# A seven-product matmul scheme with running PSUM sums, and seven quarter products for one of its products

## Chip, cores and metric

The kernel runs on one core of a Trainium2 chip. The metric is device time in microseconds, from the first to the last instruction with what lies around it; smaller is better. All matmuls are fp32.

## The reference

Threshold attention over 8 batches x 8 heads of 576 tokens (head size 64), then a routed two-layer network over 4608 tokens: 512 to 1024 to 512 features, 8 experts, each token with one expert.

```python
scores = scale * np.matmul(q, k.transpose(0, 1, 3, 2))
thresh = np.max(scores, axis=-1, keepdims=True) - tau
scores = np.where(scores >= thresh, scores, -1000000000.0)
attn = softmax(scores)                      # exp and division by the sum + 1e-9
x = (attn @ v) as (4608, 512)
expert_idx = token_ids * 2654435761 % 8
out[mask_e] = np.maximum(x[mask_e] @ w1[e], 0.0) @ w2[e]
```

The lines on softmax and on x are shortened here. The change touches the last line alone.

## The kernel before

**Stages.** The first half is attention, with the first layer of expert 0 done in its gaps. The expert stage follows: layer 2 of expert 0, then layers 1 and 2 of experts 1 to 7. Experts are taken in order of their number of tokens; each has a fixed number of places, 544 for expert 0, 576 for experts 1 to 4, 600 for 5 to 7 (caps). Activations are kept with features on partitions and tokens along the free side, so a weight block is the stationary operand of a matmul and half of the tokens (272, 288 or 300 columns; 240 in layer 2 of expert 7, whose other 120 tokens are done by last_tile) the moving one.

**Seven products.** Each layer is cut in 2 x 2 blocks (rows of w, columns of w, halves of the tokens), and seven (line 926) makes it of seven block products in place of eight. Four sums of weight blocks (left: s1 to s4) and four of activation blocks (right: t1 to t4) are made first by VectorE; s1 overwrites a21, t1 overwrites b12. The products are a11 b11, a12 b21, s2 t2, s3 t3, a22 t4, s1 t1, s4 b22. Each goes to a fresh pair of PSUM banks (bank2, line 851, which alternates between two pools of two pairs each), and VectorE adds it to what was added before: ScalarE copies p1 to SBUF, VectorE makes c11, u2, u3, c21, u4, c22 and c12, seven adds, and ScalarE applies the ReLU in layer 1. Layer 1 runs seven for two groups of 256 output features (14 products of 4 fp32 matmuls); layer 2 runs it once (7 products of 8). Every fp32 matmul is a pair of instructions in the trace, so a product shows as x8 or x16. In the profile L941 is the matmul of seven, L951 the copy of p1, L948 the ReLU, L861 the helper add (the seven adds, and s1), L858 the helper sub (the other sums of blocks).

**Operands.** In layer 1 the 128 columns of a weight block lie side by side (w1_blocks). In layer 2, except for expert 7, the features are dealt (dealt, line 877): output feature m of block i comes from every fourth column of w_sb, so a stationary operand reads fp32 values 16 bytes apart, and from w_s, the sums, 8 bytes apart. Dealt features let VectorE transpose the result oT in 32 x 32 squares into o_q (put_squares, line 1024), from which POOL writes rows of the output by indirect DMA.

**Order around it.** The order of instructions on each engine is the written one (manual_schedule). seven calls a hook after each output or sum (after): side1 in layer 1 (line 1085), side2 in layer 2 (line 1099). The hooks deal out VectorE's other work: sums of w2 and h for the coming layer 2 (w2_work, h_work), sums of w1 and x for the next expert (x_work), the squares of the next expert's x (turn_x, line 1052: five transpositions into xq, then 16 DMAs on SP that carry xq to xT), put_squares; and POOL's gathers (fetch), SP's weight loads (load_w1, load_w2). At the end put_out and last_tile write expert 7's rows.

Of the kernel before, what the change touches and what calls it, by code (L numbers as in the profile page):

```python
# [20 lines left out]
def kernel(  # L21
# [805 lines left out]
    with tc.tile_pool(name="m_x", bufs=1) as m_x, \  # L827
         tc.tile_pool(name="m_o", bufs=3) as m_o, \
# [9 lines left out]
        o_end = m_x.tile([P, DIN], FP32, name="o_end")  # L838
# [6 lines left out]
        halves = [m_s.tile([P, 2, CH], FP32, name=n) for n in ("p1", "u2", "u3", "u4")]  # L845
# [3 lines left out]
        turn = [0]  # L849

        def bank2():
            turn[0] ^= 1
            if turn[0]:
                return ps_sc.tile([P, 2, 512], FP32, name="sc")
            return ps_m.tile([P, 2, 512], FP32, name="bank2")
# [53 lines left out]
        def sums_w2(e):  # L909
            s1 = None  # L910
            if e == E - 1:
                spare = w_pool.tile([P, CO, F], FP32, name="w1_sb")
                s1 = w_tiles["s1"] = spare[:, :, 0:D2]
            return left(*w2_blocks(e, w_tiles[e, 2]), w2_sums(e), s1)
# [11 lines left out]
        def seven(a, a_s, b, b_s, m0, outs, relu, after):  # L926

            (a11, a12, s1, a22), (s2, s3, s4) = a, a_s
            (b11, t1, b21, b22), (t2, t3, t4) = b, b_s
            c11, c12, c21, c22 = outs  # L930
            n_k, width, dealt_out = a11.shape[1], b11.shape[2], len(a11.shape) == 4
            p1, u2, u3, u4 = (t[:, :, 0:width] for t in halves)

            def product(x, y):
                ps = bank2()
                for i in range(2):
                    c0 = m0 + P * i
                    for c in range(n_k):
                        lhsT = (x[:, c, :, i] if dealt_out else
                                x[:, c, c0:c0 + P])  # L940
                        nc.tensor.matmul(ps[:, i, 0:width], lhsT=lhsT, rhs=y[:, c],  # L941
                                         start=c == 0, stop=c == n_k - 1)
                return ps[:, :, 0:width]

            def out(c, ps, u, step):
                add(c, ps, u)()
                if relu:
                    nc.scalar.activation(c, c, AF.Relu)  # L948
                after(step)

            nc.scalar.copy(p1, product(a11, b11))  # L951
            out(c11, product(a12, b21), p1, 0)
# [244 lines left out]
```

## Time and profile before

| | us |
|---|---|
| median of 3 runs | 931.19 (930.16 to 933.33) |
| profiled execution | 931.3 |
| its span | 929.7 |
| expert stage in it: first product of layer 2 of expert 0 to last_tile | 501.02 to 914.19 |
| one layer of experts 1 to 4 without waits (14 x 1.94 or 7 x 3.88) | 27.16 |
| one layer of experts 5 to 7 without waits (layer 2 of expert 7 is shorter) | 28.28 |

The page gives the busy time of each engine and, in 40 slices of 23 us, its share in tenths; a group line gives line of the code, engine, operation, operands, shapes and count, then total, mean ns and idle time before it; a timeline line gives start, length, engine, line, operands and count, and in brackets how long the engine stood before it and for whom. PEld is the weight load, which runs ahead beside PE. Lengths of matmuls are longer than their pitch, as they overlap: times per product are taken from start to start.

### The profile page before, as it was taken

Reading aid. Unit: us, or ns where it says so; the run is one execution under the profiler, and the core shown is the slowest. Engines: PE = TensorE matmul, PEld = TensorE weight load, DVE = VectorE, ACT = ScalarE, POOL = GpSimd, SP = SyncE. Lnnn points to the kernel's source line nnn. Section 1 sums busy time; section 2 is a strip of 40 time slices with the busy share of each in tenths; the row PEclk is TensorE's granted clock in tenths of the full one; section 3 lists DMA queues with packets and bytes.
Section 4 is the critical chain, followed back from the end, with each engine's and each line's share of the span. In section 5 each row is a group of like instructions: output and inputs, shape, how many; then the busy total and the mean of one; then the engine's idle time right before and its main releaser. Section 6 shows DMA issues by size and latency. Waiting matters only on the chain.

```text
span 929.7 us, 20725 instructions
## 1 busy us (share of the span) xinstructions
PE 909.8 (98%) x7495; PEld 662.0 (71%) x7495; DVE 757.5 (81%) x1654; ACT 457.3 (49%) x741; POOL 403.7 (43%) x528
## 2 busy tenths in 40 slices
PE   7999999999999999999999999999999999999996
PEld 4666666656666566665678888788887978878785
DVE  7999999999999999999955776767668676777551
ACT  6888888888888898888812010110201021020110
POOL 4232432456666623455423370724527073440702
PEclk9999999999999999999999999999999999999999
DMA  7354463554545668743101745364372536412101
GB/s 175 92 148 118 109 152 93 136 131 103 123 105 153 159 165 214 216 107 88 30 25 51 237 131 158 133 173 141 95 223 75 164 133 165 157 34 50 48 3 55
DMA packets 114775, 113.11 MB, mean 122 GB/s; under 512 B 32475, under 2 KB 89315, under 8 KB 114672
## 3 DMA queue, kind: packets, MB, share of 16 engines
q1 hardware_dynamic: 105168, 92.64, 37.0%
q0 software_dynamic: 9072, 18.91, 7.0%
q8 instruction: 61, 1.00, 0.4%
q14 instruction: 42, 0.34, 0.1%
q10 hardware_dynamic: 432, 0.21, 0.1%
HBM read 81.99 MB, written 21.44 MB: 111 GB/s over the span
## 4 chain that ended last, share of the span: by engine, by line
PE 65%; issue 21%; POOL 7%; DVE 3%; ACT 2%; DMA 1%; another core or an unknown queue 1%; POOLq 0%; SPq 0%; DVEq 0%; ACTq 0%
PE av L313 18%; PE sc L235 15%; PE tr L282 11%; PE sc L941 9%; PE bank L941 8%; POOL out_dram L1036 6%; PE sc L640 2%; PE av L282 1%; POOL xg L119 1%; ACT w L260 1%; DVE ns L246 1%; DVE w L271 1%; ACT wT_b L303 1%; ACT wT_a L303 0%
## 5 line engine op out<-in xcount | busy, mean ns | idle before, releaser
L260 ACT ACTIVATE w<-ns,nmx 128x576 f32<-128x576 f32 x288 | 220.5, 777 | 28.8 <-DVE ns L246 27.8
L271 DVE SCALAR_TENSOR_TENSOR w<-ns,thr,w 128x576 f32<-128x576 f32 x288 | 225.8, 816 | 0.0
L1036 POOL DMA_INDIRECT out_dram<-o_q,qidx x127 | 138.1, 1087 | 191.7 <-DVE o_q L1028 153.1
L246 DVE TENSOR_SCALAR_CACHE_REDUCE ns<-sc 128x576 f32<-128x576 f32 x288 | 205.6, 747 | 8.1 <-PE sc L235 7.4
L253 POOL TENSOR_SCALAR thr<-nmx,drop 128x2 f32<-128x2 f32 (+1 forms) x160 | 104.4, 653 | 187.3 <-DVE ns L246 177.6
L235 PE MATMUL sc<-k_sb,q 64*128 64x288 f32 (+1 forms) x1280 | 179.2, 423 | 1.0 <-DVE drop L704 0.7
L282 PEld LDWEIGHTS tr<-ident,w 64*128 64x128 f32 x2624 | 106.0, 138 | 95.4 <-ACT wT_b L303 32.4
L282 PE MATMUL tr<-ident,w 64*128 64x64 f32 x2624 | 139.5, 231 | 6.0 <-ACT wT_b L303 2.6
L948 ACT ACTIVATE h<-h 128x576 f32<-128x576 f32 (+1 forms) x56 | 38.7, 693 | 164.8 <-DVE h L861 126.1
L235 PEld LDWEIGHTS sc<-k_sb,q 64*128 64x128 f32 (+1 forms) x1280 | 93.0, 177 | 23.2 <-DVE ns L246 9.4
L313 PE MATMUL av<-wT_a,v 128*64 128x320 f32 (+1 forms) x704 | 100.6, 418 | 0.2
L303 ACT COPY wT_a<-tr 128x512 f32<-128x512 f32 (+1 forms) x128 | 81.7, 638 | 20.7 <-PE tr L282 20.2
L303 ACT COPY wT_b<-tr 128x512 f32<-128x512 f32 (+1 forms) x128 | 81.4, 636 | 17.1 <-PE tr L282 11.2
L313 PE MATMUL av<-wT_b,v 128*64 128x256 f32 x640 | 83.2, 389 | 0.0
L313 PEld LDWEIGHTS av<-wT_a,v 128*64 128x64 f32 x704 | 43.8, 137 | 29.3 <-DVE xm L352 0.7
L951 ACT COPY p<-bank 128x576 f32<-128x576 f32 (+2 forms) x11 | 7.0, 633 | 99.5 <-PE bank L941 72.5
L313 PEld LDWEIGHTS av<-wT_b,v 128*64 128x64 f32 x640 | 40.2, 136 | 18.8 <-issue 0.7
L542 POOL DMA_INDIRECT slot_scratch<-tok,slot_i x36 | 45.0, 1251 | 9.4 <-issue 7.6
L941 PE MATMUL bank<-h,w_sb 128*128 128x288 f32 (+3 forms) x192 | 48.1, 404 | 0.0
L941 PE MATMUL sc<-h,w_sb 128*128 128x288 f32 (+3 forms) x192 | 47.7, 401 | 0.0
L941 PEld LDWEIGHTS bank<-h,w_sb 128*128 128x128 f32 x192 | 46.6, 300 | 0.5
L941 PEld LDWEIGHTS sc<-h,w_sb 128*128 128x128 f32 x192 | 45.9, 289 | 0.6
(197 smaller groups left out, 1303.7 us busy)
## 6 DMA issues: line engine op xcount, KB each, us to landing
w_sb<-in_moe_w_dram SPq DMA_DIRECT2D x16, 2048.0 KB
q<-in_q_dram SPq DMA_DIRECT2D x62, 288.0 KB
v<-in_v_dram SPq DMA_DIRECT2D x32, 256.0 KB
x_scratch<-xm SPq DMA_DIRECT2D x32, 256.0 KB
xT<-xq SPq DMA_DIRECT2D x84, 80.0 KB
k_sb<-in_k_dram SPq DMA_DIRECT2D x31, 144.0 KB
k_sb<-in_k_dram SPq DMA_DIRECT2D x32, 112.0 KB
x_scratch<-xg SPq DMA_DIRECT2D x9, 256.0 KB
```

Of the source, the lines that this page charges most:

```text
L235: nc.tensor.matmul(sc[out_rows, i, 0:S2], lhsT=q_sb[rows, h, q0:q1], rhs=k_sb[rows, h], start=True, stop=True)
L246: nc.vector.tensor_scalar(out=ns[:].rearrange("p (i s) -> p i s", i=2), in0=sc[:, :, 0:S2], scalar1=-1.0, scalar2=None, op0=ALU.mult, op1= ...
L253: nc.gpsimd.tensor_scalar(out=thr[:, 0:j + 1], in0=stats[n][0][:, 0:j + 1], scalar1=drop[:], scalar2=None, op0=ALU.add)
L260: nc.scalar.activation(w, nss[n, j][:], AF.Exp, bias=stats[n][0][:, j:j + 1], scale=-1.0)
L271: nc.vector.scalar_tensor_tensor(out=w, in0=nss.pop((n, j))[:], scalar=stats[n][1][:, j:j + 1], in1=w, op0=ALU.is_le, op1=ALU.mult, accum_ ...
L282: nc.tensor.transpose(dst[:, r, 64 * c:64 * c + 64], src[rows, c0:c0 + P], ident[rows, rows])
L303: nc.scalar.copy(dst, tr[:, :, 0:64 * n_c].rearrange("p r (c q) -> p r c q", c=n_c))
L313: nc.tensor.matmul(av[64 * j:64 * j + 64, g, c0:c1], lhsT=v_sb[:, c, 64 * j:64 * j + 64], rhs=wT[g][:, i, c0:c1], start=(c == 0), stop=stop)
L542: nc.gpsimd.indirect_dma_start(out=slot_dram[c % 2][:, :], out_offset=bass.IndirectOffsetOnAxis(ap=slot_i[:, c:c + 1], axis=0), in_=tok[:, ...
L941: nc.tensor.matmul(ps[:, i, 0:width], lhsT=lhsT, rhs=y[:, c], start=c == 0, stop=c == n_k - 1)
L948: nc.scalar.activation(c, c, AF.Relu)
L1036: inst = nc.gpsimd.indirect_dma_start(out=rows[:, :], out_offset=bass.IndirectOffsetOnAxis(ap=idx, axis=0), in_=o_sb, in_offset=None, boun ...
```

## The change

Three things. First, the seven products are not each put in a fresh pair of banks: p1, u2, u3 and c21 are successive states of one pair x, onto which the products accumulate, and s1 t1 and c12 of another pair z; ScalarE copies x to SBUF after p1, u2 and u3 (u3 by halves), VectorE adds only c11, c22 and c12. The banks are four fixed pairs (banks). Second, in experts 1 to 7 the product a12 b21 is made by a class Quarters of seven products of its quarters (half the columns, half the inner rows): in layer 1 for both groups at once, in layer 2 of one output chunk each. Each of these products is 2 fp32 matmuls of half width in both layers. Their sums wi_s and bi_s are made by VectorE in the hooks, ScalarE copies their p1, s1 t1, u2 and c21 out, VectorE adds the other three results, and the whole is written into the place of c11, to which p1 is added later (join; in the second group of layer 1 first(False) adds the product from PSUM). Third, the hooks are numbered anew and deal out the work in other portions; o_sb and o_end give way to the buffers xg_bufs.

What is left out: bi_sums, inner_w, inner_b and second_blocks (views of quarters, and left and right on them), the body of the old seven, two lines on buffers of output rows and the overflow loop's output buffer.

```diff
-        o_end = m_x.tile([P, DIN], FP32, name="o_end")
...
-        halves = [m_s.tile([P, 2, CH], FP32, name=n) for n in ("p1", "u2", "u3", "u4")]
+        halves = [m_s.tile([P, 2, CH], FP32, name=n) for n in ("p1", "u2", "u3")]
+        wi_s = m_s.tile([P, 3, D2], FP32, name="wi_s")
+        bi_s = m_s.tile([P, 3, CH], FP32, name="bi_s")
+        quarters = [m_s.tile([P, CH], FP32, name=n) for n in ("q_p1", "q_u2", "q_p5")]
...
-        turn = [0]
-        def bank2():
-            turn[0] ^= 1
-            if turn[0]:
+        banks, turn = [], [0]
+        def late_tile(fo):
+            if fo in (2, 4):
                 return ps_sc.tile([P, 2, 512], FP32, name="sc")
             return ps_m.tile([P, 2, 512], FP32, name="bank2")
+        def bank2():
+            turn[0] += 1
+            return banks[(turn[0] - 1) % 4]
...
+                w_tiles["s1_q"] = spare[:, 0:2, D2:D2 + P]
...
+        def products(ps, x, y, start, mid=None):
+            for i, lhsTs in enumerate(x):
+                for c, lhsT in enumerate(lhsTs):
+                    nc.tensor.matmul(ps[:, i], lhsT=lhsT, rhs=y[:, c], start=start and c == 0,
+                                     stop=c == len(lhsTs) - 1, skip_group_check=not start)
+                if i == 0 and mid:
+                    mid()
+        def columns(x, m0=0, n=2):
+            if len(x.shape) == 4:
+                return [[x[:, c, :, i] for c in range(x.shape[1])] for i in range(n)]
+            return [[x[:, c, m0 + P * i:m0 + P * i + P] for c in range(x.shape[1])]
+                    for i in range(n)]
+        class Seven:
+            def __init__(self, a, a_s, b, b_s, m0, outs, relu, x, z):
+                self.a = [columns(t, m0) for t in (*a, *a_s)]
+                self.b, self.outs, self.relu = (*b, *b_s), outs, relu
+                width = b[0].shape[2]
+                self.x, self.z = x[:, :, 0:width], z[:, :, 0:width]
+                self.p1, self.u2, self.u3 = (t[:, :, 0:width] for t in halves)
+            def evict(self, c, src):
+                if self.relu:
+                    nc.scalar.activation(c, src, AF.Relu)
+                elif src is not c:
+                    nc.scalar.copy(c, src)
+            def out(self, c, ps, u):
+                add(c, ps, u)()
+                self.evict(c, c)
+            def first(self, keep=True):
+                products(self.x, self.a[0], self.b[0], True)
+                if keep:
+                    nc.scalar.copy(self.p1, self.x)
+                else:
+                    self.out(self.outs[0], self.x, self.outs[0])
+            def second(self, y):
+                y = y[:, :, 0:self.x.shape[2]]
+                products(y, self.a[1], self.b[2], True)
+                self.out(self.outs[0], y, self.p1)
+            def join(self):
+                self.out(self.outs[0], self.outs[0], self.p1)
+            def u2_sum(self):
+                products(self.x, self.a[4], self.b[4], False)
+                nc.scalar.copy(self.u2, self.x)
+            def s1_t1(self):
+                products(self.z, self.a[2], self.b[1], True)
+            def u3_sum(self):
+                products(self.x, self.a[5], self.b[5], False)
                 for i in range(2):
+                    nc.scalar.copy(self.u3[:, i], self.x[:, i])
+            def c22(self):
+                self.out(self.outs[3], self.z, self.u3)
+            def c21(self):
+                products(self.x, self.a[3], self.b[6], False)
+                self.evict(self.outs[2], self.x)
+            def c12(self, mid=None):
+                products(self.z, self.a[6], self.b[3], False, mid)
+                self.out(self.outs[1], self.z, self.u2)
+        class Quarters:
+            def __init__(self, a, a_s, b, b_s, outs, n, x, y, z):
+                self.a = [columns(t, 0, n) for t in (*a, *a_s)]
+                self.b, self.outs = (*b, *b_s), outs
+                width = b[0].shape[2]
+                self.x, self.y, self.z = (t[:, :, 0:width] for t in (x, y, z))
+                self.p1, self.u2, self.p5 = (
+                    t[:, 0:n * width].rearrange("p (i t) -> p i t", i=n) for t in quarters)
+            def p1_p2(self):
+                products(self.x, self.a[0], self.b[0], True)
+                nc.scalar.copy(self.p1, self.x)
+                products(self.y, self.a[1], self.b[2], True)
+                add(self.outs[0], self.y, self.p1)()
+            def s1_t1(self):
+                products(self.z, self.a[2], self.b[1], True)
+                nc.scalar.copy(self.p5, self.z)
+            def u2_sum(self):
+                products(self.x, self.a[4], self.b[4], False)
+                nc.scalar.copy(self.u2, self.x)
+            def c12(self):
+                products(self.z, self.a[6], self.b[3], False)
+                add(self.outs[1], self.z, self.u2)()
+            def c22(self):
+                products(self.x, self.a[5], self.b[5], False)
+                add(self.outs[3], self.x, self.p5)()
+            def c21(self):
+                products(self.x, self.a[3], self.b[6], False)
+                nc.scalar.copy(self.outs[2], self.x)
+        def w_quarters(a):
+            if len(a.shape) == 4:
+                return [a[:, 2 * j:2 * j + 2, :, i:i + 1] for i in range(2) for j in range(2)]
+            k, m = a.shape[1] // 2, a.shape[2] // 2
+            return [a[:, k * j:k * j + k, m * i:m * i + m] for i in range(2) for j in range(2)]
+        def wi_sums(a):
+            return [wi_s[:, i].rearrange("p (k m i) -> p k m i", k=2, i=1) if len(a.shape) == 4
+                    else wi_s[:, i].rearrange("p (k m) -> p k m", k=a.shape[1] // 2)
+                    for i in range(3)]
...
+        def quarters_of(e, layer, x, y, z):
+            a, b = second_blocks(e, layer)
+            t = b.shape[2] // 2
+            if layer == 1:
+                outs = [h_0[:, 2 * i:2 * i + 2, t * k:t * k + t] for i in range(2) for k in range(2)]
+            else:
+                outs = [oT[:, i:i + 1, t * k:t * k + t] for i in range(2) for k in range(2)]
+            a_q = w_quarters(a)
+            if (e, layer) == (E - 1, 2):
+                a_q[2] = w_tiles["s1_q"]
+            return Quarters(a_q, wi_sums(a), b_quarters(b), bi_sums(b), outs,
+                            3 - layer, x, y, z)
         def layer1(e, side):
-            w, half = w_tiles.pop((e, 1)), caps[e] // 2
-            for g in range(NG):
+            w, half = w_tiles[e, 1], caps[e] // 2
+            def group(g, x, z):
                 outs = [h_0[:, FH * i + 2 * g:FH * i + 2 * g + 2, half * k:half * k + half]
                         for i in range(2) for k in range(2)]
-                seven(w1_blocks(w), triple(w1_s, 0, C2), x_blocks(e), triple(x_s, 0, C2, half), 2 * P * g,
-                      outs, True, lambda step: side(g, step))
+                return Seven(w1_blocks(w), triple(w1_s, 0, C2), x_blocks(e),
+                             triple(x_s, 0, C2, half), 2 * P * g, outs, True, x, z)
+            q = quarters_of(e, 1, *banks[1:])
+            g0, g1 = group(0, banks[0], banks[2]), group(1, banks[1], banks[3])
+            w_tiles.pop((e, 1))
+            g0.first()
+            side(0)
+            q.p1_p2()
+            q.s1_t1()
+            g0.u2_sum()
+            side(1)
+            q.u2_sum()
+            q.c12()
+            g0.u3_sum()
+            side(2)
+            q.c22()
+            g0.c21()
+            side(3)
+            q.c21()
+            g0.s1_t1()
+            g0.c22()
+            g0.join()
+            side(4)
+            g1.first(False)
+            g0.c12()
+            side(5)
+            g1.u2_sum()
+            side(6)
+            g1.s1_t1()
+            side(7)
+            g1.u3_sum()
+            g1.c22()
+            side(8)
+            g1.c21()
+            side(9)
+            g1.c12()
         def layer2(e, side):
...
             a = w2_blocks(e, w)
...
                 a[2] = w_tiles["s1"]
-            seven(a, w2_sums(e), h_blocks(0, FH, half),
-                  triple(h_s, 0, FH, half), 0, outs, False, side)
+            o = Seven(a, w2_sums(e), h_blocks(0, FH, half), triple(h_s, 0, FH, half), 0, outs,
+                      False, banks[0], banks[1])
+            q = quarters_of(e, 2, banks[2][:, 0:1], banks[2][:, 1:2], banks[3][:, 0:1]) if e else None
+            o.first()
+            if q:
+                q.p1_p2()
+            else:
+                o.second(banks[2])
+            side(0)
+            o.u2_sum()
+            side(1)
+            if q:
+                q.s1_t1()
+                q.u2_sum()
+            o.s1_t1()
+            side(2)
+            if q:
+                q.c12()
+                q.c22()
+            o.u3_sum()
+            o.c22()
+            if q:
+                q.c21()
+                o.join()
+            side(3)
+            o.c21()
+            o.c12(lambda: side(4))
+            side(5)
         def last_tile(middle):
-            w, o_sb, idx = w_tiles[E - 1, 2], o_end, gidx[:, KT - 1:KT]
+            w, o_sb, idx = w_tiles[E - 1, 2], xg_bufs[KT - 1], gidx[:, KT - 1:KT]
...
-            late_h(lambda fo: (ps_sc.tile([P, 2, 512], FP32, name="sc") if fo in (2, 4) else
-                               ps_m.tile([P, 2, 512], FP32, name="bank2")))
+            late_h(late_tile)
+            for _ in range(2):
+                banks += [ps_sc.tile([P, 2, 512], FP32, name="sc"),
+                          ps_m.tile([P, 2, 512], FP32, name="bank2")]
...
                 if e > 0:
+                    a, b = second_blocks(e, 2)
                     w2_work, h_work = sums_w2(e), sums_h(e, 0, 2)
-                    def side1(g, step):
-                        if g == 0:
+                    w2_work += inner_w(a, None if more else w_tiles["s1_q"])
+                    def side1(step):
+                        if step == 0:
+                            put_squares(e - 1, 1)
+                        elif step < 5:
                             run(w2_work)
-                            if step == 0:
-                                put_squares(e - 1, 1)
-                        else:
+                        elif step < 7:
+                            run(w2_work, 2)
+                        if step > 5:
                             run(h_work)
-                        if step > 2:
-                            run(turns, 1 if g == 0 else 2)
+                        if step > 3:
+                            run(turns)
                     layer1(e, side1)
-                    run(sums_h(e, 2, FH), 4)
-                x_work = (sums_w1(e + 1) + sums_x(e + 1)) if more else []
+                    run(sums_h(e, 2, FH) + inner_b(b), 8)
+                x_work = []
+                if more:
+                    x_work = sums_w1(e + 1) + sums_x(e + 1)
+                    a, b = second_blocks(e + 1, 1)
+                    x_work += inner_w(a) + inner_b(b)
                 def side2(step):
                     if step == 0:
                         run(turns, len(turns))
                     else:
-                        run(x_work, 2)
+                        run(x_work, (2, 3, 3, 8, 0)[step - 1])
                     if step == 2 and e + 2 < E:
                         fetch(e + 2)
                     if step == 4 and e + 2 < E:
                         load_w1(e + 2)
-                    if more and step == 3:
+                    if more and step == 4:
                         put_squares(e, 0)
                     if not more and step == 4:
                         put_out(e, (0,))
```

More of the change, by code (lines that the diff above doesn't have):

```diff
@@ L827 @@
     with tc.tile_pool(name="m_x", bufs=1) as m_x, \
-         tc.tile_pool(name="m_o", bufs=3) as m_o, \
          tc.tile_pool(name="m_s", bufs=1) as m_s:
@@ L924, in run @@
                 work.pop(0)()
[L926 to L935, printed above, removed]
-                for i in range(2):
[L937 to L952, printed above, removed]
-            add(u2, product(s2, t2), p1)()
-            after(1)
-            add(u3, product(s3, t3), u2)()
-            after(2)
-            out(c21, product(a22, t4), u3, 3)
-            k5 = product(s1, t1)
-            add(u4, k5, u2)()
-            out(c22, k5, u3, 4)
-            out(c12, product(s4, b22), u4, 5)
@@ new lines, in b_quarters, with bi_sums, inner_w, inner_b @@
+        def b_quarters(b):
+            k, t = b.shape[1] // 2, b.shape[2] // 2
+            return [b[:, k * j:k * j + k, t * i:t * i + t] for j in range(2) for i in range(2)]
+        def bi_sums(b):
+            k, t = b.shape[1] // 2, b.shape[2] // 2
+            return [bi_s[:, i, 0:k * t].rearrange("p (k t) -> p k t", k=k) for i in range(3)]
+        def inner_w(a, s1=None):
+            return left(*w_quarters(a), wi_sums(a), s1)
+        def inner_b(b):
+            return right(*b_quarters(b), bi_sums(b))
@@ new lines, in second_blocks @@
+        def second_blocks(e, layer):
+            if layer == 1:
+                return w1_blocks(w_tiles[e, 1])[1], x_blocks(e)[2]
+            return w2_blocks(e, w_tiles[e, 2])[1], h_blocks(0, FH, half2(e))[2]
+        def quarters_of(e, layer, x, y, z):
+            a, b = second_blocks(e, layer)
+            t = b.shape[2] // 2
+            if layer == 1:
+                outs = [h_0[:, 2 * i:2 * i + 2, t * k:t * k + t] for i in range(2) for k in range(2)]
[6 more added lines that the diff above has]
+                            3 - layer, x, y, z)
@@ L1014, in put_out @@
                     rows = rows_of(kt)
-                    o_sb = m_o.tile([P, DIN], FP32, name="o_sb")
+                    o_sb = xg_bufs[kt]
                     dst = o_sb[0:rows].rearrange("p (c r q) -> p r c q", c=CO, r=2)
@@ L1159 @@
                                  start=(fo == 0), stop=(fo == FO - 1))
-            o_sb = m_o.tile([P, DIN], FP32, name="o_sb")
+            o_sb = xg_bufs[1]
             nc.scalar.copy(o_sb[:], o_ps[:, 0])
```

## The prediction

> **What bounds the kernel now.** I read the page's busy times and slices first, then the waits of TensorE in the expert stage, then its timeline product by product, then the groups of weight loads, and last the hand-overs between engines.
>
> ```profile
> PE 909.8 (98%) x7495; PEld 662.0 (71%) x7495; DVE 757.5 (81%) x1654; ACT 457.3 (49%) x741; POOL 403.7 (43%) x528
> ...
> DVE  7999999999999999999955776767668676777551
> ACT  6888888888888898888812010110201021020110
> ```
>
> TensorE is busy at nine tenths from the second slice to the last but one; VectorE drops to five to seven tenths in the expert stage (from slice 22), ScalarE to one. So TensorE sets the time there, and VectorE's adds cost nothing while they are on time.
>
> ```profile
> PE bank L941 <- DVE h_s L858: 1.9, 2, 1.6
> PE sc L941 <- ACT p L951: 0.6, 1, 0.6
> PE bank L941 <- ACT p L951: 0.5, 1, 0.5
> ```
>
> Waits of TensorE from 495 to 925 us (total, times, longest). The start times of the products give a fuller figure: 98 products of layer 1 and 56 of layer 2 run from 501.02 to 914.19, 413.2 us; each has a pitch (below), their sum is 407.9, so 5.3 us are lost: 2.0 and 0.6 at the start of layer 2 of experts 1 and 3, 1.4 and 1.3 in layer 1 of experts 6 and 7. No more than 5.3 can come from waits.
>
> ```profile
> 501.02 3.90 PE L941 MATMUL sc<-h,w_sb 128*128 128x272 f32 x16
> 504.76 3.90 PE L941 MATMUL bank<-h,w_sb 128*128 128x272 f32 x16
> 508.49 3.83 PE L941 MATMUL sc<-h_s,w_s 128*128 128x272 f32 x16
> 512.16 3.83 PE L941 MATMUL bank<-h_s,w_s 128*128 128x272 f32 x16
> 515.83 3.90 PE L941 MATMUL sc<-h_s,w_sb 128*128 128x272 f32 x16
> 519.57 3.91 PE L941 MATMUL bank<-h,w_sb 128*128 128x272 f32 x16
> 523.32 3.83 PE L941 MATMUL sc<-h,w_s 128*128 128x272 f32 x16
> 526.98 2.10 PE L941 MATMUL bank<-xT,w_sb 128*128 128x288 f32 x8
> ```
>
> Expert 0, 272 columns: seven products of 8 fp32 matmuls, each two instructions (x16). Start to start, the products that load from w_sb last 3.74 us, 233.6 ns an instruction (1st, 2nd, 5th, 6th); those from w_s 3.67, or 229.4. That difference is the key of this forecast.
>
> ```profile
> L941 PEld LDWEIGHTS bank<-xT,w_sb 128*128 128x128 f32 x168 | 31.9, 190 | 9.5
> ...
> L941 PEld LDWEIGHTS sc<-h_s,w_sb 128*128 128x128 f32 x64 | 15.8, 310 | 0.2
> L941 PEld LDWEIGHTS sc<-h,w_s 128*128 128x128 f32 x80 | 15.5, 195 | 3.0
> ```
>
> Mean weight load: 190 ns where the 128 columns lie side by side (layer 1), 195 where they lie 8 bytes apart (w_s of layer 2), 310 where they lie 16 bytes apart (w_sb of layer 2, which is used four columns apart).
>
> ```profile
> 914.39 0.66 DVE L861 TENSOR_TENSOR oT<-sc,u 128x480 f32<-128x480 f32 x1 [2.61 <-PE sc L941]
> ...
> 920.41 1.91 PE L990 MATMUL sc<-w_sb,h 128*120 128x128 f32 x16
> ```
>
> 16 instructions of 128 columns: last start 1.91 - 0.273 = 1.64 us after the first, 109 ns each. Elsewhere the pitch is 242.5 ns at 288 columns, 252.5 at 300, 202.5 at 240: 2.5 + 0.833 per column, which gives 109.2 at 128. So 144, 150 and 120 columns cost 122.5, 127.5 and 102.5, if the load keeps up.
>
> ```profile
> 512.62 10.66 SPq L1064 DMA_DIRECT2D xT<-xq  x16
> ...
> 524.76 0.76 DVE L858 TENSOR_TENSOR x_s<-xT 128x576 f32<-128x576 f32 x1 [4.27 <-DMA xT<-xq]
> ```
>
> Expert 0's squares are sent by SP from 512.62, and VectorE stands 4.27 us until they have landed, at 524.76, before its first sum of x.
>
> ```profile
> 571.65 4.04 PE L941 MATMUL bank<-h_s,w_sb 128*128 128x288 f32 x16
> 571.85 0.76 DVE L861 TENSOR_TENSOR u<-sc,u 128x576 f32<-128x576 f32 x1 [0.73 <-PE sc L941]
> ...
> 585.23 2.10 PE L941 MATMUL bank<-xT,w_sb 128*128 128x288 f32 x8
> 585.47 0.64 ACT L951 COPY p<-sc 128x576 f32<-128x576 f32 x1 [22.63 <-PE sc L941]
> ```
>
> VectorE starts 0.20 us, ScalarE 0.24 us after TensorE has begun the next product; from a vector's end to the waiting matmul it took 0.06 (564.69 to 564.75).
>
> **What the skill says.** "SBUF — State Buffer", section "Door 1: The DMA port swizzle": lines are 16 bytes, and at least two accesses to a line are needed for full speed. The loads agree: 195 ns at two per line, 310 at one. "TensorE: Matmul & The Clock Gate", section "LDWEIGHTS (loading the stationary operand)": the time goes with the number of columns; the trace has 183 ns at 120 and 190 at 128. So halving the moving side doesn't make the load shorter. The same page, "Architectural detail": VectorE and ScalarE are strict FIFO, only weight loads are pulled ahead. The 4.27 us above agree. "PSUM — Partial Sum Buffer", section "The four PSUM rules": a synchronised read in the middle of an accumulation is allowed. No run here shows one yet.
>
> **Columns.** In each layer of experts 1 to 7, 16 instructions of full width become 28 of half width.
> - Layer 1 (loads side by side): 16 x 242.5 = 3.88 becomes 28 x 122.5 = 3.43, -0.45 for experts 1 to 4; 4.04 becomes 3.57, -0.47 for 5 to 7. Sum -3.2.
> - Layer 2 of experts 1 to 6: four of the seven quarter products (a11, a12, s1, a22) still load w_sb 16 bytes apart; the three from wi_s are dense. An instruction's step is the longer of its own columns and the next one's load. In the written order 15 steps have a strided load next (7 in p1 and p2, 3 in s1 t1, 1 before the outer s1 t1, 4 in c21), 13 haven't: 15 x 233.6 + 13 x 122.5 = 5.10 against 3.88: +1.22 for experts 1 to 4, and 5.16 against 4.04, +1.12, for 5 and 6. Sum +7.1.
> - Expert 7's layer 2 isn't dealt: 28 x about 109 against 16 x 202.5: -0.1 or -0.2.
> Sum of the columns +3.8. Were the strided load hidden, layer 2 would give -2.7 instead, and the columns -6.1.
>
> **Waits in expert 0 and at its end.** The third item of side2's step 2 is now the first sum of x, and stands before c22's add in VectorE's queue. The squares land at 524.76 as before (the steps up to them keep their place). So c22's add runs at 525.5 to 526.2; the last product accumulates onto the bank it reads and waits to 526.3, instead of 523.3: +3.0. Before, the new product had a free bank. Behind the add stand three sums of x (2.4), eight quarter sums (0.43 each at 256 elements and 0.32 at 144, read off the line through 0.757 at 576 and 1.214 at 1024: 3.2 with gaps) and the transposition into o_q (2.0): c12's add starts at 533.9, ends at 534.6. Expert 1's q.p1 uses that bank, and would start at 531.9: +2.7. Bounds for the two: 3 if the squares come early, 7 if late. I take 5.7. SP and POOL: the squares' 16 DMAs are issued as before; load_w1 and the fetch keep their steps; put_squares(e, 0) goes one product later, POOL's rows with it, which it has room for (43% busy).
>
> **Waits in layer 1.** Each add or copy that now stands between two matmuls of a bank, with the work put between: after u2_sum, the copy needs 0.24 + 0.63 + 0.06 = 0.93, cover two quarter products, 0.98: just hidden. The copies of u3 are by halves, so c21 finds the first half free: hidden, if waits go by the half (if not, +0.6 to +1.1 a group). g0.c22: 1.02 under g1.first's 1.94: hidden. g1.first's add isn't: VectorE has c22 (0.67), the join (0.78), a w2 sum (1.2) and a square (0.65) ahead of it, then 0.7: 0.2 + 4.0 + 0.06 = 4.3 against two products, 3.88: +0.4 (0 to 0.65), seven times: 2.8. At the start of experts 2 to 7, q.p1 waits for layer 2's c12 add: behind c22's add at 20.4 us of the layer come join, three x sums, eight quarter sums and o_q's transposition, so that it ends at 30.3, where TensorE arrives (28.4 + 1.94): +0.1 (0 to 0.35), six times: 0.6. In layer 2 I find none.
>
> **What goes.** VectorE loses four adds a group and gains quarter adds and sums: about even, and off the path. The 5.3 us of TensorE's waits came from late starts of VectorE and ScalarE that nothing in the profile explains (up to 4.5 us, releaser "remote" or "issue"). They may vanish (-5.3) or, with shorter cover and three times as many ScalarE instructions, hit harder (+9). I take +2.
>
> **The end.** last_tile's first bank is now that of the last product's z, and waits for c12's add: 0.2 + 0.66 + 0.06 = +0.9; before, the line at 914.39 ran beside it. o_q and o_sb from other buffers: nothing, as they are read out long before.
>
> **Sum.** 3.8 + 5.7 + 2.8 + 0.6 + 2.0 + 0.9 = +15.8 on the profiled execution's own 931.3 us (span 929.7; the median shown is 931.19, so no shift): 947.
>
> **Rivals.**
> - Columns alone set the time: the interleaving covers all waits and the load keeps pace with 122 ns. For it: no product at 288 columns shows the stride. Against it: the 233.6 of expert 0. It gives -6.1 - 5.3 + 0.9: 921 to 925. It decides from a pitch of strided loads under 152 ns (where layer 2 breaks even: (3880 - 13 x 122.5)/15) and less than 3 us of waits. Faster, 0.12.
> - Loads hidden, waits as above: 931.3 + 15.8 - 9.9 = 937; or loads as above and waits half: 940. Near the forecast's lower side, 0.18; with the 5.3 gone as well, within 0.3% (under 934): 0.07.
> - Waits go by the whole tile, or late engines hit every layer: 14 layers at 1 us more, 955 to 965: 0.15.
> - The quarters don't come into play at all (the shorter form is not used): excluded by the code, e > 0 takes them in both layers.
> - Forecast, 942 to 953: 0.48.
>
> 0.3% (2.8 us) is about what a measurement of this kernel can tell from no change. Faster 0.12, same 0.07, slower 0.81. Range 934 to 959: it leaves out the faster cases and most of the last rival.
>
> **What would show it.** In the timeline of the new kernel: layer 2's quarter instructions at 234 ns where they load w_sb, at 122 where they load wi_s; layer 1's all at 122; a gap of 3 us before expert 0's last product, and one near 2.7 after expert 1's first; 0.4 us before g1.u2_sum in each layer 1; 0.9 before last_tile. Wrong if strided short instructions run at 122 ns, or if TensorE's idle total in the stage stays near 5.

## Result and profile after

The changed kernel takes 992.44 us at the median of four executions (981.32, 987.96, 996.93, 1001.86), the kernel before 930.80. Ratios in this document leave out executions that are over 1.5% above the fastest of their kernel: here two are left, with a mean of 984.64, and the ratio is 1.0573 [1.0504, 1.0643]. The change makes the kernel slower, as forecast, but by some 53 us (61.6 at the median of all four) where 15.8 were forecast, and the time lies outside the range of 934 to 959. The profiled execution is the longest of the four, 17 us above that mean, so its gaps are larger than those behind the ratio; the traces of e1 and e2 below show gaps of the same kind.

The page after: busy times, and of the 40 slices those of TensorE, with the granted clock.

```profile
PE 936.9 (94%) x7663; PEld 680.3 (68%) x7663; DVE 758.9 (76%) x1720; ACT 505.1 (50%) x864; POOL 406.4 (41%) x528
...
PE   8999999999999999999988899898977979989996
...
PEclk9999999999999999999999899899998989999999
```

TensorE has gained 27 us of busy time, yet its share has sunk from 98 to 94%, and from the 21st slice on the row varies between 7 and 9. The clock row, at 9 throughout attention, has four 8s in the expert stage: for part of these slices less than the full clock was granted. So next come the waits of TensorE in that stage (total, times, longest).

```profile
PE bank L935 <- DVE h L865: 13.1, 4, 6.2
PE sc L935 <- ACT q_p L1016: 9.1, 7, 4.4
PE bank L935 <- ACT h L1038: 5.7, 2, 3.5
```

Before, no releaser cost more than 1.9 us. Two kinds are mixed here: seven waits for the copy q_p, once an expert, and a few long ones, up to 6.2 us, for VectorE and ScalarE. The timeline of layer 1 of expert 4 shows a long one (start, length, engine, line, operands; in brackets the idle time before and for whom).

```profile
737.59 2.10 PE L935 MATMUL sc<-xT,w_sb 128*128 128x288 f32 x8
...
741.81 2.21 PE L935 MATMUL bank<-xT,w_sb 128*128 128x288 f32 x8 [2.12 <-ACT h L1038]
...
744.24 0.98 POOL L1220 DMA_INDIRECT out_dram<-o_q,qidx  x1 [0.30 <-issue]
745.53 0.98 POOL L1220 DMA_INDIRECT out_dram<-o_q,qidx  x1 [0.30 <-issue]
745.66 0.76 DVE L865 TENSOR_TENSOR h<-sc,u 128x576 f32<-128x576 f32 x1 [7.71 <-remote]
...
746.47 2.21 PE L935 MATMUL sc<-xT,w_s 128*128 128x288 f32 x8 [2.45 <-issue]
...
754.05 0.76 DVE L865 TENSOR_TENSOR h<-bank,h 128x576 f32<-128x576 f32 x1 [5.21 <-remote]
...
754.86 3.87 PE L935 MATMUL bank<-x_s,w_s 128*128 128x288 f32 x8 [6.18 <-DVE h L865]
```

TensorE's product s1 t1 starts at 737.59, and its record ends at 739.69. VectorE's add of c22, which needs it, starts only at 745.66, after 7.71 us of idleness that the trace puts down to a signal from elsewhere ("remote"). TensorE waits in turn: the product c12 at 746.47 accumulates onto the bank that this add reads until 746.42 (the trace names no releaser for it). The same comes again at 754.05: g1's first product is over at 744.02, VectorE's add of it starts 10 us later, after 5.21 us of idleness, and u2_sum at 754.86 starts right behind the add. Meanwhile GpSimd sends a row write every 1.29 us. The next view gives stretches of the same time: length, busy times of PE, PEld, DVE, ACT and POOL, then the granted clock, the DMA share and GB/s.

```profile
731.00:739.30 8.30, 7.95 (x42) 6.45 (x40) 3.35 (x5) 1.64 (x4) 6.44 (x7) 1.00 0.15 49
739.30:751.00 11.70, 4.80 (x18) 2.88 (x16) 3.18 (x4) 2.40 (x4) 8.96 (x10) 1.00 0.16 50
751.00:758.40 7.40, 3.54 (x8) 2.59 (x9) 4.28 (x8) 1.35 (x2) 1.71 (x2) 0.54 0.15 43
```

TensorE is busy nearly throughout the first, loses time in the second, and has a clock of 0.54 in the third. DMA is busy at 0.15 or 0.16 in all three, so the amount of transfers doesn't tell them apart. The clock records show seven phases of half clock in the stage, of 3.41 or 6.83 us, each in or just behind a gap. The Trainium skill has this ("TensorE: Matmul & The Clock Gate", section "Part 1: The HAM clock gate"): after an idle window of about 3.4 us the clock falls to half, and one busy window brings it back. The lengths agree, one or two times 3.41 us; but the gap before the first phase, from 522.96 to 525.21, was 2.25 us only, so here a shorter gap than the page's was enough.

**One account for all runs.** For every matmul instruction of the stage I took the time to the next one's start and set against it 2.5 ns + 0.833 ns per column; what is over is lost to half clock (where it was granted) or to waits and strided loads. "Late" counts signals of TensorE's semaphore recorded more than 0.9 us after the instruction's end. In the quiet runs the latest came 0.02 us after it. In the runs with late signals 13 to 29 of the stage's 155 to 232 signals have no record of their own, so these counts are rough. The signals of VectorE and ScalarE that are recorded in the same runs came within 0.01 us of the instruction's end: TensorE's alone are late. Capital letters are the chips that the runs fell on; the row of after (A) is of the longest of its executions.

| run (chip) | stage | own columns | half clock | waits, loads | late |
|---|---|---|---|---|---|
| before (A) | 413.2 | 407.5 | 0 | 5.7 | 20 |
| after (A) | 485.1 | 401.2 | 14.2 | 69.7 | 16 |
| e1 running sums only (B) | 491.5 | 407.5 | 16.2 | 67.8 | 18 |
| e2 both quarters, fresh banks (B) | 480.4 | 401.2 | 20.2 | 59.0 | 11 |
| e3 layer 1 quarters, fresh banks (B) | 424.3 | 404.3 | 1.6 | 18.5 | 30 |
| e4 after, no row writes (B) | 438.5 | 401.2 | 0 | 37.3 | 0 |
| e5 after, ten memsets (C) | 496.4 | 401.2 | 11.8 | 83.4 | 0 |
| e6 before, ten memsets (C) | 493.5 | 407.5 | 11.0 | 75.1 | 0 |
| e7 before, no row writes (C) | 408.0 | 407.5 | 0 | 0.5 | 0 |
| e8 as e2, order mended (C) | 457.9 | 401.2 | 4.7 | 52.0 | 27 |
| e9 after, four memsets (D) | 438.8 | 401.2 | 0 | 37.7 | 0 |
| e10 before, four memsets (D) | 408.7 | 407.5 | 0 | 1.2 | 0 |
| e11 as e9, waits covered (D) | 438.9 | 401.2 | 3.1 | 34.7 | 0 |
| e12 layer 1 quarters, four memsets (D) | 410.9 | 404.3 | 1.6 | 5.1 | 0 |
| e13 after (E) | 438.4 | 401.2 | 0 | 37.3 | 0 |
| e14 as e9 (E) | 438.6 | 401.2 | 0 | 37.5 | 0 |
| e15 as e4 (E) | 439.0 | 401.2 | 0 | 37.8 | 0 |
| e16 as e12, from expert 2 (E) | 405.8 | 404.7 | 0 | 1.1 | 0 |

The kernel before has late signals too (some 20 of them in the first profile), but on A its fresh banks hid most of them: 5.7 us were lost. In the changed kernel they stand on TensorE's path.

### The profile page after: what moved, and what is told of

Same layout as the page of the kernel before. It is cut to its first block, busy times and chain, and to the rows that moved or that the text cites. A ratio compares the mean times of both kernels' runs of the same rounds, so it can differ in the third digit from the quotient of the medians.

```text
span 1000.2 us, 21275 instructions
## 1 busy us (share of the span) xinstructions
PE 936.9 (94%) x7663; PEld 680.3 (68%) x7663; DVE 758.9 (76%) x1720; ACT 505.1 (50%) x864; POOL 406.4 (41%) x528
## 4 chain that ended last, share of the span: by engine, by line
PE 46%; issue 35%; POOL 13%; ACT 2%; DMA 2%; DVE 1%; POOLq 0%; SPq 0%; ACTq 0%; DVEq 0%
PE av L313 17%; PE sc L235 14%; PE tr L282 10%; POOL out_dram L1220 10%; POOL xg L119 3%; PE sc L640 2%; DMA out_dram<-o_q,qidx 2%; PE av L282 1%; ACT w L260 1%; ACT wT_b L303 1%; DVE ns L246 0%; ACT wT_a L303 0%; PE sc L658 0%; DMA k_sb<-in_k_dram 0%; DVE w L271 0%
## 5 line engine op out<-in xcount | busy, mean ns | idle before, releaser
L1220 POOL DMA_INDIRECT out_dram<-o_q,qidx x127 | 135.1, 1064 | 247.9 <-DVE o_q L1212 209.5
L958 ACT ACTIVATE h<-h 128x576 f32<-128x576 f32 (+1 forms) x42 | 28.9, 693 | 77.4 <-DVE h L865 63.9
L935 PE MATMUL sc<-h_s,w_s 128*128 128x288 f32 (+3 forms) x256 | 67.1, 417 | 0.0
L935 PEld LDWEIGHTS sc<-h_s,w_s 128*128 128x128 f32 x256 | 51.4, 205 | 11.0
L935 PE MATMUL sc<-h,w_sb 128*128 128x288 f32 (+6 forms) x200 | 49.2, 399 | 9.1 <-ACT q_p L1016 9.1
L119 POOL DMA_INDIRECT xg<-x_scratch,gidx_x x35 | 39.7, 1134 | 38.3 <-DVE xq L1240 30.3
L991 ACT COPY u<-sc 128x288 f32<-128x288 f32 (+3 forms) x30 | 10.5, 402 | 80.8 <-PE sc L935 78.9
```

The costliest lines, as they stand in the source:

```text
L119: nc.gpsimd.indirect_dma_start(out=dst, out_offset=None, in_=src, in_offset=bass.IndirectOffsetOnAxis(ap=idx, axis=0), bounds_check=src.sh ...
L935: nc.tensor.matmul(ps[:, i], lhsT=lhsT, rhs=y[:, c], start=start and c == 0, stop=c == len(lhsTs) - 1, skip_group_check=not start)
L958: nc.scalar.activation(c, src, AF.Relu)
L1220: inst = nc.gpsimd.indirect_dma_start(out=rows[:, :], out_offset=bass.IndirectOffsetOnAxis(ap=idx, axis=0), in_=o_sb, in_offset=None, boun ...
```

## The experiments

**First: is it the running sums or the quarters, and what makes the signals late?** Four kernels on chip B. e1 makes a12 b21 plainly again.

```diff
-            q.p1_p2()
-            q.s1_t1()
+            g0.second(banks[1])
             g0.u2_sum()
```

> The product a12 b21 is again one plain product, in both layers; the sums running in PSUM stay. Theory A (each product of a running sum has to wait for the copy or add that reads its own bank, and every late start of VectorE or ScalarE now lands on TensorE): nearly all of the loss stays, 965 to 990 us, with TensorE waiting 40 us or more in the expert stage. Theory B (the short quarter products and their extra copies, adds and strided weight loads are the loss): 932 to 942 us.

1009.02 us, 1.0775 [1.0732, 1.0818]: beyond theory A's range, on the side away from B. The loss is all there without a quarter product, so the short products are not the main cause. That it is larger than the changed kernel's on A may be the chip, or that each quarter product was also cover for a copy; the runs don't separate these.

e2 keeps the quarters and puts each product in a fresh bank, VectorE adding in SBUF.

```diff
-                products(self.x, self.a[4], self.b[4], False)
-                nc.scalar.copy(self.u2, self.x)
+                add(self.t[1], full(self.a[4], self.b[4]), self.t[0])()
```

> The quarters of both layers stay, the running sums go: each product has a fresh pair of banks out of four and its sum is made by VectorE in SBUF, as before the change. Theory A: 934 to 945 us, the 3.8 us of columns and a few us of waits, since a fresh bank is read three products before it is needed. Theory B: 970 us or more.

999.22 us, 1.0677 [1.0638, 1.0717]: a miss for theory A, but in part made by the experiment: layer 2's sums of weight quarters were written into wi_s ahead of layer 1's last quarter products, so that these computed something else, and TensorE waited 4 and 2 us for VectorE in each layer 1. e8 below mends it.

e3 is the same scheme with quarters in layer 1 only (QL = (1,)).

> Fresh banks as in the run with both layers' quarters, but quarters in layer 1 alone (weights side by side). Columns alone give -3.2 us: 928 us, 926 to 934 with the shorter cover. The distance to the run with both layers' quarters is the price of the strided weight loads in layer 2: +7 us by the forecast's term.

946.91 us, 1.010 [1.0062, 1.0137]: 18.5 us of waits. Some are by late signals, of which there are 30; others stand at one place of layer 1, up to 0.83 us ahead of the quarters' c12 in experts 1 to 5. My reading is that four banks in rotation with quarters between come round sooner than before, and that late signals get through fresh banks as well; how much of the miss against 928 is due to each, this run doesn't tell.

e4 takes GpSimd's writes out of the changed kernel.

```diff
-            for s in range(s0, s1):
-                put_rows(o_q[i][:, s - s0].rearrange("p a c -> p (a c)"), qidx[:, e, s:s + 1],
-                         rows=out_q)
```

> The changed kernel without GpSimd's indirect writes of the rows of experts 0 to 6 (their rows of the output are left out; the transpositions into o_q stay). If these writes delay the signals between the engines: the late starts go, 955 to 970 us, and TensorE's waits fall from 70 to about 40 us. If not: 980 to 1002 us as the changed kernel.

964.61 us, 1.0307 [1.0286, 1.0327]. No signal is late and no clock is halved. What remains, 37.3 us, is nearly the same in every expert. Its whole time is 7 us too long for the stage (22.6 us after the stage in place of 15.6), so the stage is what to compare. The changed kernel with its writes was not run on B; there e1 to e3 are the runs with writes.

**Second: the number of writes, or their pace?** On chip C. e5 and e6 put memsets behind each write, in the changed kernel and in the one before.

```diff
+                for _ in range(10):
+                    nc.gpsimd.memset(pause[:], 0.0)
```

> The changed kernel with GpSimd's row writes spread: after each of the 127 writes ten small memsets on a tile that nothing reads (about 1 us), so that a write is issued every 2.3 us or so instead of every 1.29. Theory P (the late starts come from a backlog that the burst of 18 writes at this pace builds up): 962 to 972 us, TensorE's waits about 40 us, no half clock. Theory Q (each write costs the signals something, whatever the pace): the loss stays, 985 us or more.

> The kernel before with the same memsets between the row writes. Theory P: the late starts go here too, and as fresh banks hid all but about 5 us of them, 926 to 931 on the chip of the first runs, that is 0.995 of the kernel before. Theory Q: 1.00 or more.

1029.72 (1.0993 [1.0945, 1.104]) and 1030.70 (1.0991 [1.0943, 1.1038]): both misses in time. The timeline of e5 says why.

```profile
656.73 0.98 POOL L1223 DMA_INDIRECT out_dram<-o_q,qidx  x1 [0.63 <-issue]
...
660.12 0.98 POOL L1223 DMA_INDIRECT out_dram<-o_q,qidx  x1 [0.63 <-issue]
...
662.61 2.21 DVE L1213 STREAM_TRANSPOSE o_q<-oT 128x1152 f32<-128x1152 f32 x1 [11.82 <-issue]
...
668.14 1.33 PE L936 MATMUL bank<-bi_s,w_sb 128*128 128x144 f32 x4 [7.53 <-DVE h L866]
```

A write now leaves every 3.39 us, and 18 of them no longer fit into an expert. VectorE's transposition into o_q stands 11.82 us. The trace names no releaser here; in the whole run it puts 71.8 us of six such waits down to these writes. VectorE's adds stand behind, and TensorE 7.53 us behind these. This is a queue that I overfilled. Yet no signal was late, so the pace of the writes does bear on it, at least on this chip.

e7 is the kernel before without the writes (same cut as e4).

> The kernel before without GpSimd's row writes of experts 0 to 6 (those rows of the output are left out). What it gains is what the late starts cost it: 0.994 to 0.997 of the kernel before if fresh banks hide them nearly all; the distance to the changed kernel without row writes is then the price of the columns and of the waits that are the same in every expert, 30 to 38 us.

933.31 us, 0.9956 [0.9937, 0.9975], and a stage without a wait (0.5 us): with the writes gone, nothing is left that TensorE waits for. The ratio fell into the expected range partly by luck, as 22.2 us follow the stage here, 6.7 more than in the first profile; the stage itself gained more. The kernel before was not profiled on B and C. From its medians, with some 501 us ahead of the stage and 15.5 behind it as in the other traces, its stage took about 419 us on B and 421 on C, an estimate: 12 to 14 us lost, so fresh banks hid less there than on A. e4's stage less e7's, on two chips, is 30.5 us, the steady price of the change.

e8 is e2 with inner_w moved to the second group's hooks.

```diff
-                            run(w2_work, 2 if step > 2 else 1)
+                            run(w2_work, 1 if step < 4 else 0)
...
                             run(h_work)
+                            run(w2_work, 1 if step < 4 else 0)
```

> Quarters in both layers with fresh banks and VectorE's sums, as in the run that had them before, but the sums of layer 2's weight quarters come after the last quarter product of layer 1 has read the tile that they share (in that run they came before it, and VectorE's queue then held up TensorE by 4 and 2 us in every layer 1). Theory A: 940 to 955 us. If 985 or more stays, fresh banks do not help once quarters shorten the time until a bank comes round again.

974.36 us, 1.0321 [1.0236, 1.0405]: between the two expectations, with 27 late signals. Its stage is 27 us under that of the profiled changed kernel (on another chip), and still 50 over e7's on the same one. VectorE is busy at 85% in this run and has the quarters' adds as well. Four of its waits, 1.5 to 1.6 us each, come at one place of layer 2 in four experts, for VectorE's sum h_s, which points to VectorE's queue. As this form was not run without late signals, how its 52 us divide between late signals and VectorE's own work stays open.

**Third: a pace that fits, and the steady waits.** On chip D. e9 and e10 are e5 and e6 with range(4): a write every 2.3 us.

> The changed kernel with four memsets after each row write: a write every 2.3 us or so. At ten memsets it was 3.4 us; no signal of TensorE was late by over 0.9 us, but 18 writes no longer fitted into an expert's time and VectorE's transposition into o_q, and behind it TensorE, waited 7 to 16 us for them. Theory P (backlog of a burst): 965 to 972 us, TensorE's waits 37 to 45 us, no half clock. Theory Q (each write costs something at any pace): 985 us or more.

> The kernel before with the same four memsets. Theory P: as fast as without the row writes, 0.994 to 0.998 of the kernel before. Theory Q: 1.00 or more.

949.70 (1.0335 [1.0319, 1.0351]) and 919.46 (1.0005 [0.9997, 1.0014]). In e9 the waits of 37.7 us and the full clock are as theory P wants, in e10 the time isn't: nothing was there to gain. The kernel before takes 919.05 on this chip, not 931 to 939, and that raised the doubt that the fourth set takes up.

e11 covers four of the steady waits.

```diff
             q.c22()
+            g0.s1_t1()
+            g0.c22()
             g0.c21()
...
-banks[2][:, 0:1], banks[2][:, 1:2], banks[3][:, 0:1])
+banks[2][:, 0:1], banks[3][:, 1:2], banks[3][:, 0:1])
...
-                        run(x_work, (2, 3, 3, 8, 0)[step - 1])
+                        run(x_work, (2, 2, 4, 8, 0)[step - 1])
```

In layer 2, q.c12 also changes places with u3_sum and c22.

> As the changed kernel with four memsets, and with four of its waits met: layer 2's p2 in a tile other than p1's, two quarter products instead of one between u3's copies and c21 in layer 2, group 0's s1 t1 there in layer 1, and the first sum of x behind the add of c22 in expert 0. Theory W (these waits come from tiles that are tracked whole, and from cover that is too short): 13 to 17 us less than the run with four memsets alone, by the gaps in the trace without row writes (0.52, 0.64 + 0.23 and 0.30 + 0.23 in seven experts each, 1.7 in expert 0). If the gaps only move to the next product: 0 to 5 us less.

948.43 us, 1.3 less than e9: a miss. The waits of TensorE in e11:

```profile
PE bank L936 <- DVE oT L866: 6.3, 7, 3.5
PE bank L936 <- ACT u L992: 5.6, 7, 0.8
PE bank L936 <- ACT h L1039: 3.9, 7, 0.6
```

The waits for q_p are gone, and those for u are down to one an expert and one in expert 0; every wait that I moved cover to is met. But s1 t1 had been cover for q.c21's copy, which now holds up g1.first by 0.70 in seven experts (ACT h), and the later sums of x delay layer 2's last add, which holds up the next expert's first quarter product by 3.5 us once and 0.5 to 0.7 six times (DVE oT); the 3.5 us then cost 3.1 us of half clock. A product used as cover in one place is missing in another.

e12 has quarters in layer 1 only, fresh banks, four memsets, and g1's first product ahead of the last two quarter products.

> Quarters in layer 1 alone, fresh banks, four memsets after a row write, and group 1's first product put before the last two quarter products so that their banks are free. If the waits that are left (1.5 us in each layer 1 of the earlier run) go, the columns' 3.2 us come out and it beats the kernel before: 0.989 to 0.995 of it. If they stay, 0.998 to 1.006.

920.89 us, 1.0025 [1.0016, 1.0033]. Of the 6.7 us that it loses in the stage, nearly all stands at the start of expert 1 (1.28 and 3.02 us of waits, then 1.6 of half clock), where VectorE still has that expert's sums to make.

**Fourth: the chip, or the pace?** On chip E, side by side: the changed kernel, e9 and e4 again.

> The changed kernel as it is, on one chip with the next two. Theory P (burst of row writes delays signals): late starts as before, 1.05 to 1.08 of the kernel before. If the chip made them: 1.03 to 1.04, like the run with four memsets.

> The changed kernel with four memsets after each row write, again. Theory P: 1.031 to 1.036 of the kernel before, 20 us or more under the changed kernel on the same chip. If the chip decides: equal to it within 0.5%.

> The changed kernel without the row writes of experts 0 to 6 (these rows of the output are left out), again. Theory P: within 0.4% of the run with four memsets, since these keep the signals on time. If the writes cost something at any pace: 1% or more below it.

950.08 (1.0338 [1.0323, 1.0353]), 949.30 (1.0327 [1.0312, 1.0342]) and 956.78 (1.0409 [1.0394, 1.0424], again 7 us of it after the stage). Theory P as I had put it fails: in this run a write every 1.29 us delays nothing. The waits of the unaltered changed kernel here:

```profile
PE bank L935 <- ACT u L991: 5.6, 7, 0.8
PE sc L935 <- ACT u L991: 3.6, 9, 0.8
PE bank L935 <- DVE oT L865: 3.2, 2, 1.8
PE sc L935 <- ACT q_p L1016: 2.6, 7, 0.4
```

The long waits are gone, the copies' waits have stayed. So the burst of writes is needed for late signals, but isn't enough. On B they vanish without the writes, on C with a slower pace or without writes; on E there are none in the full burst. D and F were profiled at 2.3 us a write only, without late signals; that the kernel before, with its burst, takes the same 919 us there as on E suggests that they are like it. I put the difference down to the chip. But A, B and C came first and D, E and F later, and none was visited twice, so the runs don't separate the chip from the time.

e16 leaves the quarters out of expert 1.

```diff
-            q = quarters_of(e, 1) if 1 in QL else None
+            q = quarters_of(e, 1) if 1 in QL and e > 1 else None
```

> Quarters in layer 1 of experts 2 to 7 alone, fresh banks, four memsets after each row write. In the run that had them from expert 1 on, 4.5 of the 5.3 us of waits and all of the half clock (1.55) stood at the start of expert 1. Without that, six times 0.45 us of columns is left as a gain: 0.996 to 0.999 of the kernel before. 1.00 or more if the start of expert 1 isn't what held it.

916.00 us, 0.9967 [0.9955, 0.9978]: it beats both kernels. Its stage is 2.9 us under e10's, where six experts' columns make 3 x 0.45 + 3 x 0.47 = 2.8.

Two runs more, e9's and e16's kernels on chip F, were to show the pace of 2.3 us where signals are late.

> The changed kernel with four memsets after each row write, once more. On a chip whose kernel before takes 930 us or more, theory P (the burst delays the signals there) expects no late signals and 1.015 to 1.03 of the kernel before, as that has late signals itself and this hasn't; theory Q 1.05 or more. On a chip at 919 us it repeats 1.033 and tells nothing.

> Layer 1 quarters of experts 2 to 7, fresh banks, four memsets, once more. On a chip whose kernel before takes 930 us or more: 0.985 to 0.993 of it if the memsets keep the signals on time, 0.997 to 1.01 if not. On a chip at 919 us: 0.996 to 0.998.

F was another quiet chip: 950.00 (1.0335 [1.0319, 1.035]) and 915.25 (0.9959 [0.9946, 0.9973]). They repeat e14 and e16 and leave the question open.

## Why the forecast was wrong

The direction was right; the size missed by some 38 us, in two steps: waits by the half of a tile, and the price of late signals. The steady part can be read from e13 against e10, two stages without a late signal (438.4 and 408.7: +29.8); e9, on e10's chip, has e13's stage within 0.4. Three places in e13:

```profile
588.31 2.12 PE L935 MATMUL sc<-x_s,w_s 128*128 128x288 f32 x8
...
590.52 0.70 ACT L991 COPY u<-sc 128x288 f32<-128x288 f32 x2 [2.05 <-PE sc L935]
...
591.27 2.21 PE L935 MATMUL sc<-x_s,w_sb 128*128 128x288 f32 x8 [0.35 <-ACT u L991]
...
615.66 0.28 ACT L1016 COPY q_p<-sc 128x144 f32<-128x144 f32 x1 [0.18 <-PE sc L935]
...
615.99 1.21 PE L935 MATMUL sc<-h,w_sb 128*128 128x144 f32 x4 [0.37 <-ACT q_p L1016]
...
620.92 0.98 PE L935 MATMUL bank<-h,w_sb 128*128 128x144 f32 x4
...
621.74 0.65 PE L935 MATMUL sc<-bi_s,wi_s 128*128 128x144 f32 x4
...
622.23 4.15 PE L935 MATMUL bank<-h,w_sb 128*128 128x288 f32 x16
```

- **Columns**: forecast +3.8. Own columns fell by 6.3 in the stage. The four strided instructions from 620.92 take 0.82 us, three steps of 234 and one of 122.5 ns; the dense ones from 621.74 take 0.49. Of the 37.3 us of the table 10.4 are such small steps, where 9.9 were reckoned: +4.1. Right.
- **Expert 0 and the start of expert 1**: forecast 3.0 + 2.7, measured 1.6 + 2.0. Right in kind: the sum of x stands ahead of c22's add.
- **g1.u2_sum**: forecast 2.8, measured 1.5. **Start of layer 1 of experts 2 to 7**: forecast 0.6, nothing. **The end**: forecast 0.9, measured 0.91.
- **"The copies of u3 are by halves, so c21 finds the first half free: hidden, if waits go by the half"**: failed. Both copies start at 590.52, after the whole product, and c21 starts at 591.27, 0.05 us after the second copy's end. In layer 1 this costs 0.52 in the first group and 0.95 in the second, 10.4 over seven experts; in layer 2 0.53 each, 3.7; in expert 0 1.2. Together 15.2 where nothing was put. The forecast had this case and its price (0.6 to 1.1 a group) as a condition, and carried it into a rival of 0.15 instead of the sum. On the forecast's own base the steady part alone, measured 29.8, gives 961, inside that rival's 955 to 965.
- **"In layer 2 I find none"**: failed. q.p2 and q.p1 use the two halves of one tile, and p2 starts at 615.99, when q_p's copy ends at 615.94: 0.64 us, and 0.23 for the instruction behind it, seven times: 5.8. e11, with another tile for p2, doesn't have it. It is the same assumption, a wait by the half, made silently. For the copies of u3 the times above fit it, but no run gave their halves tiles of their own.
- **"What goes ... I take +2"**: failed by far the most on chip A. After less e13 is 46.6 us of stage in the profiled execution (14.2 half clock, 32.4 waits), and about 29, an estimate, in the executions behind the ratio, which are 17.2 us shorter. The kernel before loses 4.5 there against e10, so late signals add about 25 us to the difference, where 2 were put. The bound of +9 supposed that a late start could cost about what it had cost before. But before, a bank was needed again three products after its own, so only a delay beyond that reached TensorE; with running sums the very next product of the pair waits for it, nearly at full length. And gaps of 3 us and more were new, so half clock came on top, which was not in the sum at all.

The steady terms add up to 4.1 + 1.6 + 2.0 + 1.5 + 0.9 + 15.2 + 5.8 = 31.1, less 1.2 for e10's own waits: 29.9, measured 29.8. The forecast corrected for the two claims about halves alone would have read 15.8 + 15.2 + 5.8 = 36.8; the rest of the 53 needs the late signals. Where there are none the change costs 3.4% (e13), on A 5.7%.

What stays open: why signals were late during a burst of GpSimd's row writes on A, B and C and not on E, whether the chip or the time makes that difference, and whether 2.3 us a write is slow enough on the first three. What was shown is that without the writes (B, C), or at 3.4 us a write (C), none is late.

## What to carry to other kernels

A scheme of accumulation in place takes away not only adds but also the slack between a product and the reuse of its bank: count that slack in microseconds, and hold against it the longest late start in the old trace, not what those starts cost there. Take it from the program's tiles, not from banks, what a copy or a product waits for, and price the pessimistic reading in the sum where the trace can't tell. When cover is moved, look at what it covered before.

## What was not expected of the hardware

- On A, B and C, and not on E, TensorE's semaphore signals came up to 10.6 us late (e1: a product is over at 612.42, the signal for its copy comes at 622.98) while GpSimd issued row writes every 1.29 us, with DMA busy at 0.16 in the stretch shown above; without these writes the latest came 0.02 us after the instruction's end. VectorE's and ScalarE's signals were not late in the same runs.
- The chips differ by more than many changes are worth: the kernel before took 930.8, 937.1 and 939.1 us on A, B and C, and 919.1 to 919.3 on D, E and F, where its executions also lie closer (917.6 to 920.4, against 931.1 to 943.5 on C). Some 7 us of this lie ahead of the stage, which begins at 493 in place of 500.
- A gap of 3.5 us in e11 was followed by half clock that cost 3.1 us, so that it cost nearly twice its length; gaps of 1.6 and 2.0 us in e13 were followed by none. In the changed kernel's profile 2.25 us were enough.
